# Quad 5 transposed by DMA, quad 8's rows moved into the first out stage, later row copies put behind the value products

## The chip, the cores and the metric

The kernel runs on one core of a Trainium2 chip. The metric is the device time of one launch in microseconds (us). The profile is of one execution: its span is counted from its first to its last instruction, and all times in it count from the start of the span.

## The reference

Eight batches of twelve heads go through a sigmoid attention over 448 positions of 64 values; the heads are put side by side as `x`, and an MLP with a SiLU follows.

```python
def _attn_ref(q, k, v):                     # each (8, 12, 448, 64)
    scores = scale * np.matmul(q, k.transpose(0, 1, 3, 2)) - np.log(S)
    attn = 1.0 / (1.0 + np.exp(-scores))
    return np.matmul(attn, v)

def _moe_ref(x, w_in, w_out):               # x (3584, 768), w_in (768, 2048), w_out (2048, 768)
    h = x @ w_in
    g = h * (1.0 / (1.0 + np.exp(-h)))
    return g @ w_out
```

Inputs and output are float32.

## The kernel before, in words

**Quads.** The work on attention is cut into 24 *quads* of four heads, three to a batch; quads 0 to 5 are batches 0 and 1, and so on. A quad's rows of `q`, `k` and `v` are loaded by POOL with a cast to 16 bits (`load`, L120; the tiles `kf`, `qf` and `vf` have three buffers each, so quad g takes the buffer of quad g - 3). For the scores, `k` and `q` are needed transposed (`kT`, `qT`, three buffers too). There are two ways to that. `pe_transpose` (L188) multiplies 14 blocks of a tensor by the identity on TensorE (PE) and has VectorE (DVE) cast the two PSUM banks, in L203. `dma_transpose` (L207) copies the rows into the order of the tile `kr` or `qr` (L211, on DVE or on POOL) and issues a DMA transpose on SP's queue (L212).

**Units and values.** A *unit* is one of a quad's seven chunks: eight score products of a burst of two units (L225) go into a pair of PSUM banks (`psc`), and ScalarE (ACT) makes the sigmoid `attnT` of them (L232). `values` (L240) multiplies a quad's seven `attnT` by its `v` (`pav`, L256, 28 matmuls), and DVE scales the two banks into `xT` (L267).

**Stages.** The order on every engine is that of the program text; nothing is reordered. In the first stage units 0 to 23 run with the first transposes and values behind them, by the table `behind` (L698). From unit 24 on, bursts of two units stand between stretches of `first_h` (L553), the products `ph` = x·w_in of batches 0 and 1 (L288); for batch 0 ACT takes the sigmoid (L302) and DVE the product into `gTr` (L303), for batch 1 ACT takes a SiLU (L307). After unit 41 the rest of `first_h` runs by itself, up to about 76 us; this part is called the h stage below. There DVE also forms sums of weights (L326, L477) and, by `by_h1`, copies the rows of quads 6, 7 and 8. After quad 8 a small copy on POOL, the *gate*, reads `qT` of quad 8 and so waits until its transpose has landed; behind it in POOL's queue stand the loads of `k` and `q` for quads 9 to 11.

Then an *out stage* and an *h_pair* alternate three times, and a last out stage ends the kernel. Out stage m forms the output of a pair of batches in sets (`out_set`, L487), each of seven products of eight matmuls (L504, called products 1 to 7 of the set, and 8 to 14 those of the next set): DVE makes the sums `S` of two blocks of `gTr` that some products take (L512, L515, L519, L525), reads each product's bank (L514 to L541, L536 and L537 both read product 6) and adds up the results in `osb`, which SP stores. Between the matmuls of a set stand bursts of two or three units of the next six quads, each followed by the values of a finished quad. During attention PSUM has three double pairs in the out stages and two single banks, which `po` takes in turn.

**Row copies in an out stage.** The list `later` holds tensors to be copied and transposed. `rows_if_any` (L591) takes one after each burst and one half way through the products behind it. In the kernel before, a quad is put on the list when the scores of the quad three before it are done (in `burst`, L749). `behind_rows` (L602) then loads the next rows: those that belong to the next stage are held back, and are loaded together behind a gate when the last quad of the stage has been transposed (L610). In h_pair the copies are made by POOL (L811).

**Loads ahead.** `after_transpose` (L635) and `after_values` (L647) issue the loads of later quads and of the weights; `load_w_in` (L150) issues a quarter of `w_in` as four DMAs.

Of the kernel before, what the change touches and what calls it, by code (L numbers as in the profile page):

```python
# [17 lines left out]
def kernel(  # L18
# [9 lines left out]
    nc = tc.nc  # L28
# [13 lines left out]
    NQB = NQ * B  # L42
# [68 lines left out]
    def new_flat(name, g):  # L111
        flat[name, g] = p3.tile([P, 2, NCH, D], F16, tag=f"{name}f", name=f"{name}f")

    def rows_in(name, g):
        b, iq = divmod(g, NQ)
        return source[name][b, 4 * iq : 4 * iq + 4].rearrange(
            "(i h) (p c) d -> (h p) i (c d)", h=2, c=NCH
        )

    def load(names, g, c0=0, c1=NCH):  # L120
        for name in names:
            if (name, g) not in flat:
                new_flat(name, g)
            nc.gpsimd.dma_start(  # L124
                flat[name, g][:, :, c0:c1].rearrange("p i c d -> p i (c d)"),
                rows_in(name, g)[:, :, c0 * D : c1 * D],
            )
# [18 lines left out]
    gate = cpool.tile([1, 1], F16, tag="gate", name="gate")  # L146
# [3 lines left out]
    def load_w_in(step):  # L150
        cols = slice(step * DFF // 4, (step + 1) * DFF // 4)
        rows = moe_w_in[:, cols].rearrange("(iq j h d) f -> h j d iq f", j=2, h=2, d=D)
        for half in range(2):
            for j in range(2):
                nc.gpsimd.dma_start(
                    w_in_sb[j * D : (j + 1) * D, half * NQ : (half + 1) * NQ, cols], rows[half, j]
                )

    def load_w_out(nh, part):
        cols = slice(nh * NO2, (nh + 1) * NO2)  # L160
        fcs = slice(part * NFC // 2, (part + 1) * NFC // 2)
        nc.gpsimd.dma_start(  # L162
            w_out_sb[:, fcs, cols],
            moe_w_out[part * DFF // 2 : (part + 1) * DFF // 2, cols].rearrange(
                "(fc p) e -> p fc e", p=P
            ),
        )

    qkT = {}

    def new_qkT(g):
        for name in ("k", "q"):
            qkT[name, g] = p3.tile([P, NCH, P], F16, tag=f"{name}T", name=f"{name}T")
# [33 lines left out]
    def dma_transpose(g, name, copy):  # L207
        if ("k", g) not in qkT:
            new_qkT(g)
        rows = p2.tile([P, NCH, 2, D], F16, tag=f"{name}r", name=f"{name}r")  # L210
        copy(rows, flat[name, g].rearrange("p j c d -> p c j d"))  # L211
        nc.sync.dma_start_transpose(  # L212
            out=qkT[name, g], in_=rows.rearrange("p c j d -> p (c j d)")
        )
# [3 lines left out]
    def scores(g, ch):  # L218
        attnT[g, ch] = p12.tile([P, 2, S], F16, tag="attnT", name="attnT")
        psc = two_banks("psc")  # L220
        for half in range(2):
            own = slice(half * HP, (half + 1) * HP)
            for j in range(2):
                rows = slice(j * D, (j + 1) * D)
                nc.tensor.matmul(  # L225
                    psc[own, j, :S],
                    qkT["k", g][rows, ch, own],
                    qkT["q", g][rows, :, own],
                    start=True,
                    stop=True,  # L230
                )
        nc.scalar.activation(attnT[g, ch], psc[:, :, :S], AF.Sigmoid, bias=bias_s, scale=QKSCALE)  # L232
# [51 lines left out]
    def h_unit(b, fc):  # L284
        ph = one_bank("ph")
        for at, cc in enumerate(pairs):
            assert b in ready or at < 4
            nc.tensor.matmul(  # L288
                ph[:, :S],
                w_in_sb[:, cc, fc * P : (fc + 1) * P],  # L290
                xT[b][:, cc, :],
                start=(at == 0),
                stop=(at == NCC - 1),
            )
            if at < NCC - 1:
                yield 189
        if fc == NFC - 1:
            h_done.add(b)
        to = gTr[:, fc, first_col(0) + b * S : first_col(0) + (b + 1) * S]
        if b == 0:  # L300
            tsig = room_x()[:, 0]
            nc.scalar.activation(tsig, ph[:, :S], AF.Sigmoid, bias=0.0, scale=ISX)  # L302
            nc.vector.scalar_tensor_tensor(  # L303
                out=to, in0=ph[:, :S], scalar=ISX, in1=tsig, op0=ALU.mult, op1=ALU.mult
            )
        else:
            nc.scalar.activation(to, ph[:, :S], AF.Silu, bias=0.0, scale=ISX)  # L307
        yield 189
# [36 lines left out]
    def x_sums(m, lo, hi):  # L345
        if lo == 0:
            for i in (1, 2, 4):
                tx[m, i] = room_x()
        of = slice(lo, hi)
        x0, x1 = ([xT[2 * m + j][:, c * NQ : (c + 1) * NQ] for c in range(2)] for j in range(2))  # L350
        for o, x, y in (
            (tx[m, 1], x1[0], x0[0]),
            (tx[m, 2], x1[1], tx[m, 1]),
            (x1[0], x1[1], x1[0]),
            (tx[m, 4], x0[1], tx[m, 2]),
        ):
            nc.vector.tensor_sub(o[:, of], x[:, of], y[:, of])
            yield
# [186 lines left out]
            store(rows1, osb[0], whole, (nc.sync, nc.sync))  # L545
        yield 163

    by_h1 = {3: 6, 6: 7, 9: 8}
    early = [h_unit(0, fc) for fc in range(2)]
    sums = w_sums()  # L550
    in_sums = w_in_sums()
# [1 line left out]
    def first_h():  # L553
        for b in range(2):
            for fc in range(NFC):
                yield from early[fc] if b == 0 and fc < 2 else h_unit(b, fc)
                if b == 0 and fc >= 10 or b == 1 and fc < 6:
                    next(in_sums)
                if b == 0:
                    continue  # L560
                if fc >= 2:
                    next(sums)
                if fc in by_h1:
                    for name in ("k", "q"):
                        dma_transpose(by_h1[fc], name, nc.vector.tensor_copy)
                    if by_h1[fc] == 8:

                        nc.gpsimd.tensor_copy(gate, qkT["q", 8][:1, 0, :1])
                        for to in (9, 10, 11):
                            load("kq", to)  # L570

    def sets(m):
        for g in range(0, NCH - 1, 2):
# [12 lines left out]
                kept, row_blocks(m - 1, g), block(m, g), row_blocks(m, g), m == B // 2 - 1  # L586
            )

    later, sums_of_x = [], []

    def rows_if_any(before, copy):  # L591
        if sums_of_x and next(sums_of_x[0], "end") == "end":
# [7 lines left out]
    held = []  # L600

    def behind_rows(g, before):  # L602
        if g + 3 >= NQB:
            return
        if g + 3 < before:
            load("kq", g + 3)
            return
        held.append(g + 3)
        if g + 1 == before:
            nc.gpsimd.tensor_copy(gate, qkT["q", g][:1, 0, :1])  # L610
            for to in held:
                load("kq", to)
            held.clear()
# [21 lines left out]
    def after_transpose(g):  # L635
        if g == 0:
            load("kq", 3)
        elif g == 1:
            load("kq", 4)
            load_w_in(0)  # L640
            load_w_in(1)
        elif g == 2:
            load("kq", 5)
        elif g == 5:
            load("kq", 8)

    def after_values(g):  # L647
        if g == 0:
            load("v", 3)
            load_w_in(2)  # L650
            load_w_in(3)
        elif g == 1:
            load("v", 4)
            load_w_out(0, 0)
            load_w_out(0, 1)
        elif g == 2:
            load("v", 5)
            load_w_out(1, 0)
            load_w_out(1, 1)
            load("kq", 6)  # L660
            load("kq", 7)
        elif g + 3 < NQB:
            load("v", g + 3)
        if g >= 2 * NQ and g % (2 * NQ) == 2 * NQ - 2:
            sums_of_x.append(x_sums(g // (2 * NQ), 0, NQ - 1))

# [17 lines left out]
    def transposes(g, name):  # L684
        pe_transpose(g, ((name, 0, 4), (name, 4, NCH)))
        if name == "q":
            after_transpose(g)

    def rounds(g, end):
        values(g, end)  # L690
        if end == NCH:
            after_values(g)

    def begin(fc, steps):
# [21 lines left out]
        18: ((transposes, 4, "q"),),  # L716
        19: ((rounds, 2, 3),),
        20: ((rounds, 2, 6),),
        21: ((begin, 0, 4),),
        22: ((rounds, 2, 7),),  # L720
        23: ((begin, 1, 4),),
    }
    for n in range(NT_B + 3):
# [16 lines left out]
    def burst(n, size=2):  # L740

        new = units[n : n + size]
        for u in new:
            scores(*u)
        with_values = values_if_any()
        for g, ch in new:
            if ch == NCH - 1:
                waiting.append(g)
                if 9 <= g + 3 < NQB:  # L749
                    later.extend(((g + 3, "k"), (g + 3, "q")))  # L750
        return with_values

    stream = first_h()
    stretch(stream, 1600)
    for n in range(NT_B + 3, 2 * NT_B, 2):
        burst(n)
        if n in (26, 30):
            transposes(5, "k" if n == 26 else "q")
        stretch(stream, 1600)
    values_if_any()  # L760
    for _ in stream:
# [5 lines left out]
    for m in range(B // 2 - 1):  # L767
# [13 lines left out]
        left, n = 0.0, 2 * NT_B * (m + 1)  # L781
# [63 lines left out]
```

## Time and profile before

| what | us |
|---|---|
| median of 3 runs | 368.9 (368.79 to 371.45) |
| the profiled execution, its time | 368.86 |
| its span | 366.9 |
| PE busy (matmuls) | 358.8 |
| DVE busy | 251.8 |
| ACT busy | 250.0 |
| POOL busy | 77.5 |
| units from 24 on with `ph` of batch 0 | 30.45 to 57.1 |
| h stage alone | 57.1 to 76.0 |
| out stage 0 | 76.0 to 123.1 |
| out stage 1 | 156.5 to 211.4 |
| out stage 2 | 244.8 to 292.0 |
| last out stage | 325.6 to the end |

Busy time is the union of an engine's instructions. In the lines of a timeline the columns are start, duration, engine, line, operation, output and inputs, shape and count; a bracket gives the idle time of the engine just before and the instruction that ended it. A line with x2 stands for two instructions, one behind the other. Lines of DMA issues give size and the time from issue to landing. From 18 to 65 us the DMA engines move 204 GB/s on the mean (bytes as written).

### The profile page before, as it was taken

How to read it: one execution, taken by the hardware profiler on the slowest of the kernel's cores; microseconds unless marked ns; L12 is line 12 of the kernel's file. 1: busy time of each engine (PE TensorE's matmuls, PEld its weight loads, DVE VectorE, ACT ScalarE, POOL GpSimd, SP SyncE). 2: the span in 40 equal slices, each digit the busy share in tenths (PEclk: the TensorE clock that was granted, in tenths of full speed). 3: DMA queues.
4: the chain of work that ended last, by engine and by line, in shares of the span. 5: the costliest groups of instructions: out<-in, count | busy, mean ns of one | idle time of the engine just before them, and what ended most of it. 6: DMA issues, size and time to landing. Idle time of an engine off the chain costs nothing.

```text
span 366.9 us, 7595 instructions
## 1 busy us (share of the span) xinstructions
PE 358.8 (98%) x3009; PEld 184.2 (50%) x3009; DVE 251.8 (69%) x458; ACT 250.0 (68%) x339; POOL 77.5 (21%) x116
## 2 busy tenths in 40 slices
PE   7999999999999999999999999999999999999995
PEld 3554445545545555555555555554555555555552
DVE  2565559957756687867675768795756677797763
ACT  4998886479999756687877856679998956640000
POOL 8566521040051082000024046000100000000000
PEclk9999999999999999999999999999999999999998
DMA  8999999987959599006779669902963120003333
GB/s 144 197 204 204 204 204 204 188 120 124 170 86 233 116 128 178 15 0 137 106 136 189 123 135 148 131 2 51 165 100 86 23 67 0 3 0 86 88 87 85
DMA packets 65858, 42.78 MB, mean 117 GB/s; under 512 B 36128, under 2 KB 62496, under 8 KB 65824
## 3 DMA queue, kind: packets, MB, share of 16 engines
q0 software_dynamic: 27072, 22.58, 42.7%
q1 hardware_dynamic: 38320, 19.34, 26.6%
q8 instruction: 23, 0.38, 0.4%
q10 hardware_dynamic: 432, 0.39, 0.3%
q14 instruction: 11, 0.09, 0.1%
HBM read 45.61 MB, written 11.01 MB: 154 GB/s over the span
## 4 chain that ended last, share of the span: by engine, by line
PE 90%; DMA 5%; DVE 2%; POOL 1%; issue 0%; ACT 0%; DVEq 0%
PE po L504 37%; PE psc L225 11%; PE pav L256 8%; PE pa L378 8%; PE pd L378 7%; PE pc L378 7%; PE ph L288 6%; DMA w_out_sb<-in_moe_w_out_dram 5%; PE pb L378 4%; PE pw L183 2%; POOL w_out_sb L162 1%; DVE xT L267 1%; DVE kT L203 1%; PE ptrq L196 1%; PE ptrk L196 0%
## 5 line engine op out<-in xcount | busy, mean ns | idle before, releaser
L232 ACT ACTIVATE attnT<-psc,bias_s 128x896 f16<-128x896 f32 x168 | 157.9, 1010 | 21.7 <-PE psc L225 21.4
L504 PEld LDWEIGHTS <-S 128*128 128x128 f16 x448 | 41.6, 98 | 35.4 <-issue 7.3
L225 PE MATMUL psc<-qT,kT 64*64 64x448 f16 x672 | 50.7, 361 | 1.3 <-ACT attnT L232 0.5
L267 DVE TENSOR_SCALAR xT<-pav 128x448 f16<-128x448 f32 x48 | 27.7, 620 | 29.7 <-PE pav L256 29.7
L124 POOL DMA_DIRECT2D vf<-in_v_dram x24 | 17.2, 717 | 132.3 <-PE pav L256 122.5
L504 PEld LDWEIGHTS <-gTr 128*128 128x128 f16 x336 | 31.2, 98 | 26.6 <-issue 7.9
L504 PE MATMUL po<-T,S 128*128 128x384 f16 x224 | 41.7, 327 | 0.0
L504 PE MATMUL po<-w_out_sb,gTr 128*128 128x384 f16 x224 | 41.5, 327 | 0.0
L378 PEld LDWEIGHTS <-w_in_sb 128*128 128x128 f16 x288 | 27.9, 98 | 26.7 <-issue 1.1
L504 PE MATMUL po<-w_out_sb,S 128*128 128x384 f16 x224 | 40.6, 326 | 0.0
L256 PE MATMUL pav<-attnT,vf 64*64 64x448 f16 x672 | 38.3, 350 | 0.5 <-DVE gTr L303 0.4
L288 PE MATMUL ph<-xT,w_in_sb 128*128 128x448 f16 x192 | 38.7, 353 | 0.1
L378 PE MATMUL pa<-xT,w_in_sb 128*128 128x448 f16 x144 | 33.1, 353 | 0.0
L225 PEld LDWEIGHTS <-kT 64*64 64x64 f16 x672 | 18.0, 104 | 28.7 <-issue 22.4
L378 PEld LDWEIGHTS <-SI 128*128 128x128 f16 x216 | 21.1, 98 | 20.0 <-issue 0.5
L256 PEld LDWEIGHTS <-vf 64*64 64x64 f16 x672 | 21.0, 107 | 13.3 <-issue 3.8
L288 PEld LDWEIGHTS <-w_in_sb 128*128 128x128 f16 x192 | 17.8, 98 | 19.1 <-issue 3.7
L394 ACT ACTIVATE part<-pa 128x448 f32<-128x448 f32 x24 | 13.1, 545 | 18.8 <-PE pa L378 17.9
L504 PE MATMUL po<-T,gTr 128*128 128x384 f16 x112 | 22.1, 327 | 0.0
L372 ACT ACTIVATE gTr<-pc 128x448 f16<-128x448 f32 x24 | 13.1, 545 | 12.8 <-DVE pc L388 12.4
L388 DVE TENSOR_TENSOR part<-pb,part 128x448 f32<-128x448 f32 x24 | 14.9, 621 | 8.3 <-ACT part L394 5.0
L186 ACT ACTIVATE m<-po 128x384 f32<-128x384 f32 x1 | 0.5, 492 | 27.7 <-PE po L504 27.7
(75 smaller groups left out, 468.6 us busy)
## 6 DMA issues: line engine op xcount, KB each, us to landing
out_dram<-osb SPq DMA_DIRECT2D x52, 192.0 KB, 3.0
vf<-in_v_dram POOLq DMA_DIRECT2D x24, 224.0 KB, 7.0
kf<-in_k_dram POOLq DMA_DIRECT2D x23, 224.0 KB, 7.4
qf<-in_q_dram POOLq DMA_DIRECT2D x23, 224.0 KB, 7.7
w_in_sb<-in_moe_w_in_dram POOLq DMA_DIRECT2D x16, 192.0 KB, 7.9
w_out_sb<-in_moe_w_out_dram POOLq DMA_DIRECT2D x4, 768.0 KB, 14.9
out_dram<-osb SPq DMA_DIRECT2D x6, 96.0 KB, 2.1
kT<-kr SPq DMA_TRANSPOSE x18, 3.8
```

Of the source, the lines that this page charges most:

```text
L124: nc.gpsimd.dma_start(flat[name, g][:, :, c0:c1].rearrange("p i c d -> p i (c d)"), rows_in(name, g)[:, :, c0 * D : c1 * D],)
L183: nc.tensor.matmul(pw, dummy[:, :P], dummy, start=True, stop=True)
L225: nc.tensor.matmul(psc[own, j, :S], qkT["k", g][rows, ch, own], qkT["q", g][rows, :, own], start=True, stop=True,)
L232: nc.scalar.activation(attnT[g, ch], psc[:, :, :S], AF.Sigmoid, bias=bias_s, scale=QKSCALE)
L256: nc.tensor.matmul(pav[half][j * D : (j + 1) * D, :S], flat["v", g][own, j, ch, :], at[own, j, :], start=(ch == 0), stop=(ch == NCH - 1),)
L267: nc.vector.tensor_scalar_mul(xT[b][:, half * NQ + iq, :], pav[half][:, :S], SX)
L288: nc.tensor.matmul(ph[:, :S], w_in_sb[:, cc, fc * P : (fc + 1) * P], xT[b][:, cc, :], start=(at == 0), stop=(at == NCC - 1),)
L372: nc.scalar.activation(gTr[:, r * NG + i, col + c * S : col + (c + 1) * S], h, AF.Silu, bias=0.0, scale=ISX)
L378: nc.tensor.matmul(to, w[:, n, i * P : (i + 1) * P], x[:, n], start=(start and n == 0), skip_group_check=not start, stop=(n == NQ - 1),)
L388: nc.vector.tensor_add(o, po, x)
L394: nc.scalar.activation(got[i, 1], bank[i, "a"], AF.Copy)
L504: nc.tensor.matmul(po[:, :NO2], a[:, fc, :], w[:, fc, :], start=(fc == 0), stop=(fc == NHC - 1))
```

## The change

Quad 5 is no longer transposed by PE behind units 26 and 30. Its two loads go out ahead of w_in's second quarter, and its rows are copied by DVE and transposed by DMA behind units 21 and 22. Quad 8 leaves `by_h1`: it stands first on the list `later`, so that its copies, its transposes and then the gate with the loads of quads 9 to 11 come in the first burst of out stage 0. And a quad is put on `later` when the *values* of the quad three before it have been issued, one burst later than before; the row copies then stand behind the two `xT` of that quad on DVE, in most places both in a row.

```diff
-    by_h1 = {3: 6, 6: 7, 9: 8}
+    by_h1 = {3: 6, 6: 7}
...
                         dma_transpose(by_h1[fc], name, nc.vector.tensor_copy)
-                    if by_h1[fc] == 8:
-
-                        nc.gpsimd.tensor_copy(gate, qkT["q", 8][:1, 0, :1])
-                        for to in (9, 10, 11):
-                            load("kq", to)
...
-    later, sums_of_x = [], []
+    later, sums_of_x = [(8, "k"), (8, "q")], []
...
     def behind_rows(g, before):
+        if g == 8:
+            nc.gpsimd.tensor_copy(gate, qkT["q", g][:1, 0, :1])
+            for to in (9, 10, 11):
+                load("kq", to)
+            return
...
         elif g == 1:
             load("kq", 4)
             load_w_in(0)
-            load_w_in(1)
         elif g == 2:
             load("kq", 5)
+            load_w_in(1)
...
         elif g + 3 < NQB:
             load("v", g + 3)
+        if 9 <= g + 3 < NQB:
+            later.extend(((g + 3, "k"), (g + 3, "q")))
...
+    def rows_of_5(name):
+        dma_transpose(5, name, nc.vector.tensor_copy)
+        if name == "q":
+            after_transpose(5)
...
-        21: ((begin, 0, 4),),
-        22: ((rounds, 2, 7),),
+        21: ((rows_of_5, "k"), (begin, 0, 4)),
+        22: ((rounds, 2, 7), (rows_of_5, "q")),
...
             if ch == NCH - 1:
                 waiting.append(g)
-                if 9 <= g + 3 < NQB:
-                    later.extend(((g + 3, "k"), (g + 3, "q")))
...
         burst(n)
-        if n in (26, 30):
-            transposes(5, "k" if n == 26 else "q")
         stretch(stream, 1600)
```

On DVE the order in the first out stage becomes as follows (kr and qr 8, then 9):

```
T, kr, T, L518, L519, qr, L326, L524, ...
... L531, L326, xT x2, kr, qr, L536, L537, L541, ...
```

On SP the transposes of quad 9 stay ahead of the stores of set 1.

## The prediction

> **What bounds the kernel now.** I read the page's shares first, then the waits by engine, then the timelines of PE, DVE, ACT and POOL around the three places that the diff touches.
>
> ```profile
> span 366.9 us, 7595 instructions
> ...
> PE 358.8 (98%) x3009; PEld 184.2 (50%) x3009; DVE 251.8 (69%) x458; ACT 250.0 (68%) x339; POOL 77.5 (21%) x116
> ...
> PEclk9999999999999999999999999999999999999998
> ```
>
> TensorE (PE) is busy for 98% of the span at the full granted clock: time comes only from PE work taken away, and is lost only where PE is made to wait. The profiled execution took 368.86 us, 1.96 more than its span and equal to the median, 368.9. I sum against 368.9. A change under 1%, some 3.7 us, is about what a measurement of this kernel can't tell from none.
>
> All times below are on the clock of the trace of before. Place one, PE timeline, the two bursts with quad 5's transposes (units 26 and 30) and a plain one:
>
> ```profile
> 32.58 0.71 PE L225 MATMUL psc<-qT,kT 64*64 64x448 f16 x8
> 33.22 0.41 PE L196 MATMUL ptrk<-ident,kf 128*64 128x128 f16 x8
> 34.00 0.36 PE L196 MATMUL ptrk<-ident,kf 128*64 128x128 f16 x6 [0.37 <-DVE gTr L303]
> 36.10 0.57 PE L225 MATMUL psc<-qT,kT 64*64 64x448 f16 x8
> ...
> 39.55 0.57 PE L225 MATMUL psc<-qT,kT 64*64 64x448 f16 x8
> 40.05 0.58 PE L196 MATMUL ptrq<-ident,qf 128*64 128x128 f16 x14
> ...
> 42.37 0.57 PE L225 MATMUL psc<-qT,kT 64*64 64x448 f16 x8
> ...
> 51.15 0.57 PE L225 MATMUL psc<-qT,kT 64*64 64x448 f16 x8
> ...
> 53.46 0.57 PE L225 MATMUL psc<-qT,kT 64*64 64x448 f16 x8
> ```
>
> From scores to scores these take 3.52 and 2.82; the plain burst with the same nine ph matmuls takes 2.31. Place two, DVE and then PE, at the end of the first set of the first out stage:
>
> ```profile
> 87.52 1.16 DVE L267 TENSOR_SCALAR xT<-pav 128x448 f16<-128x448 f32 x2 [1.47 <-PE pav L256]
> 88.81 0.56 DVE L536 TENSOR_TENSOR osb<-po,osb 128x384 f32<-128x384 f32 x1
> 89.29 0.55 DVE L537 TENSOR_TENSOR osb<-po,osb 128x384 f32<-128x384 f32 x1
> ```
>
> ```profile
> 90.71 2.11 PE L504 MATMUL po<-w_out_sb,gTr 128*128 128x384 f16 x12
> ```
>
> In an out stage po has two banks, so product 8 (the first of set 2, at 90.71) needs product 6's bank, which L536 and L537 empty by 89.84: 0.87 of slack. Place three, POOL, and the landings of the two loads behind the gate:
>
> ```profile
> 73.57 0.18 POOL L568 COPY gate<-qT 1x1 f16<-1x1 f16 x1 [14.27 <-DMA qT<-qr]
> 74.05 0.72 POOL L124 DMA_DIRECT2D kf<-in_k_dram  x1 [0.30 <-issue]
> 74.76 0.72 POOL L124 DMA_DIRECT2D qf<-in_q_dram  x1
> ```
>
> ```profile
> kf<-in_k_dram POOLq DMA_DIRECT2D x1, 224.0 KB, 4.5
> ...
> qf<-in_q_dram POOLq DMA_DIRECT2D x1, 224.0 KB, 5.0
> ```
>
> Quad 9's rows landed near 79.8, and its copies (L211, at 82.90 and 84.50) found them there.
>
> **Quad 5 by DMA: what it removes.** 28 matmuls and their 0.37 wait: (3.52 - 2.31) + (2.82 - 2.31) = 1.72 us of PE, the upper end. Four casts of about 0.53 leave DVE and two copies (0.61, spaced 0.53) come. Not all of the 1.72 arrives, because scores need one of two psc pairs and ACT frees them (0.92 per attnT, 0.44 per tsig). Followed by hand: burst 28 is due at 34.89, but its second pair is held until 35.42; burst 32 then starts at 41.1 (1.26 early) and burst 36 at 45.75 (1.13 early), where ACT has no gap from 44.60 to 49.5. I take -1.2; ends -1.7 and 0 (ACT takes it all).
>
> **Its cover.** On POOL quad 5's two loads are issued four w_in issues earlier: their rows landed at about 29.55 and 30.64 by the POOL waits that they ended, and come some 3.85 earlier (four pieces of 0.95 each), at 25.7 and 26.8. DVE is free at 25.45, so copy k runs at 25.7; behind it xT of quad 2 isn't due before 27.64. Copy q follows at 28.7. On SP nothing else is queued. The transposes go out near 26.5 and 29.4 and are needed by unit 35 at about 43.3. In quiet they land after 2.9 (at 83.59), beside loads after 7.2 to 11.9 (130.89 to 228.20): 41.3 at the latest. Zero, with 2 us of cover; ends 0 and +4.8 (rival C).
>
> **w_in's second quarter.** Behind two loads of 1.1 each and one transpose its last piece moves from 28.44 to 30.65, and with the transposes, beside which loads ran at about 86 GB/s instead of 204 (six loads, 1.38 MB, from 131 to 147), to about 32.2; by the count of ph matmuls fc 4 needs it at 33.2. The later loads lose about 3.1: (204 - 86)/204 of the 5.3 us that 0.46 MB of transposes take at that rate. The third quarter's last piece (v 3's 32.18 and four pieces) goes from 36.0 to 39.1, due 40.7; v 3 to 34.5, due 35.9; the w_out tiles cost DVE a wait inside the h stage, where it ended 3 us ahead of PE (73.06 against 76.04). Zero; ends 0 and +1.5.
>
> **Quad 8 in the first out stage.** Two copies leave the h stage (hidden there, worth nothing). In the out stage copy k stands ahead of L518 and L519, so L519 ends at 81.24 instead of 80.70; product 4, which reads its S, starts at 81.15. With about 0.1 from DVE's end to PE (the pav at 48.09 came 0.07 after its gTr): +0.25. Copy q starts at 81.16, its transpose goes out at 81.8 and lands, with no load beside it, at 84.7. The gate runs then, and the loads of 9 to 11 follow 0.48 later: kf 9 at 85.2, qf 9 at 85.9. With the landings 4.5 and 5.0 above they are there at 89.7 and 90.9.
>
> **Row copies behind values.** Both copies of quad 9 now stand between xT of quad 6 (done at 88.6 + 0.25) and L536. Copy k waits until 89.7, copy q until 90.9; L536 runs at 91.4 and L537 ends at 92.45; product 8 starts at 92.5 instead of 90.71: 1.8 in all, the 0.25 in it. Queued behind the waiting copies on DVE are L536, L537 and L541, and behind those the stores on SP, which only the osb tiles of set 2 await, later. The nearest landings give the ends: 3.4 (the first loads of the kernel) gives 0.34, 7.4 (the last of the six loads from 74.05) gives 4.2. I take 1.8, since the group of 74.05 is the same six loads on a quiet queue.
>
> The other copies have their rows, and cost only DVE time, 1.06 for a pair. Quad 10: L519 ends at 98.0 for product 11, due 98.1: +0.15. Third stage pair (quads 21 to 23): L537 ends at 259.5 for 259.60, L519 at 266.87 for 267.0: +0.1. Second out stage: xT of quad 12 ends at 173.05, both copies precede L518, and L519 ends at 175.24 where product 11 is due at 174.76: +0.55; quad 16: L528 ends at 180.7 when product 13 is due: +0.05; quad 17, one copy ahead of L519: 190.4 against 190.12: +0.35. Together +0.95, ends 0.3 and 1.5. The gates at 104.66 and 190.12 come up to 6 later, but POOL copies the first of those rows at 128.62 and 216.93, when they have lain there for some 8 us.
>
> Sum: -1.2 + 0 + 1.8 + 0.15 + 0.95 + 0.1 = +1.8; 368.9 + 1.8 = 370.7, its own range 369.6 to 371.9.
>
> The Trainium skill, page "VectorE: DVE Perf Modes", section "The three transpose paths", gives 390 ns on TensorE and 1309 ns by DMA for 128x128, which speaks against moving quad 5. Seven such blocks would be 9.2 us, both tensors in turn 18.3, ending near 44.8 and 1.5 us late: 372.2 by that estimate, a mild case of rival C below. The trace's 2.9 us for a whole seven-block transpose disagrees where DMA is quiet; only its crowded rows come near it.
>
> **The rivals.**
> B, not slower: the loads of quad 9 land in 3.4 us, as the kernel's first one did. Then product 8 loses 0.34: -1.2 + 0.34 + 0.15 + 0.95 + 0.1 = +0.3, 369.2. It decides once qf 9 lands by 89.4. For it: the queue is emptier than at 74. Against it: no pair of loads in the trace did so.
> C: the two transposes stay in flight behind each other beside a full load queue. At the median 8.4 of the crowded rows apiece they end at 26.5 + 16.8 = 43.3, at 10.8 apiece at 48.1, which is 4.8 late. In between, some +2.4: 373.1. For it: DMA is full from 10 to 65 us. Against it: in the crowded rows they overlapped.
> D: the loads of 9 land in 7.4, so product 8 loses 4.2: 370.7 + 2.4 = 373.1. For it: the last loads of the group took that. Against it: its first two didn't.
> E: ACT takes the whole gain: 371.9.
>
> **How the numbers follow.** Forecast 0.5, B 0.17, C 0.11, D 0.11, E 0.11. The likeliest time is 370.7. The range 368.5 to 373.2 holds forecast, B and E, and C and D where they are mild, leaving out under 0.2. Faster by over 1% (below 365.2) needs more than PE's 1.7: 0.02. Slower by over 1% (above 372.6) is most of C and D: 0.2. Within: 0.78.
>
> **What would show it.** No ptr rows for quad 5, and unit 42's scores about 1.2 earlier against their old 78.41; the k and q copies of quad 9 with an idle before them ended by DMA kf and qf; a PE gap at product 8 ended by DVE osb L537; gaps under 0.6 at L519's readers in the second out stage. I am wrong if PE shows no gap at product 8, or one at unit 35 ended by DMA qT.

## The result

| | us |
|---|---|
| before, median of 20 runs (beside after) | 368.73 (368.22 to 371.45) |
| after, median of 20 runs | 371.07 (370.21 to 373.66) |
| ratio | 1.007, 95% interval 1.006 to 1.008 |
| after, the profiled execution | 370.65, its span 368.7 |

The change makes the kernel 2.3 us slower. The forecast was 370.7 within 368.5 to 373.2, with a change of less than 1% as the likeliest case: the time is inside. The prediction took a change under 1% for one that can hardly be told here; with 20 runs of each the interval is 0.1% to either side, so this one can.

The profile page of after, span and busy shares:

```profile
span 368.7 us, 7543 instructions
...
PE 358.5 (97%) x2981; PEld 183.3 (50%) x2981; DVE 250.6 (68%) x456; ACT 249.6 (68%) x339; POOL 77.5 (21%) x116
...
PEclk9999999999999999999999999999999999999999
```

28 matmuls are gone and the clock is granted in full as before (1.000 on the mean, 0.997 before). The busy time of PE falls by 1.0 us up to the h stage, but by only 0.3 in all: in the h stage and in out stages 0 and 1, where the same matmuls run with new waits between them, it is 0.7 longer. The span grows by 1.8. So the cost is in the waits, and the starts of the instructions tell it better than the busy sums. PE's timeline, the lines behind 60 us that have a wait in the bracket (before had none there):

```profile
75.63 2.44 PE L504 MATMUL po<-w_out_sb,gTr 128*128 128x384 f16 x14 [0.63 <-ACT gTr L307]
...
91.75 2.11 PE L504 MATMUL po<-w_out_sb,gTr 128*128 128x384 f16 x12 [1.26 <-DVE osb L537]
...
176.32 1.31 PE L504 MATMUL po<-T,S 128*128 128x384 f16 x7 [0.36 <-DVE S L519]
...
192.06 1.47 PE L504 MATMUL po<-T,S 128*128 128x384 f16 x8 [0.16 <-DVE S L519]
```

The last three are the places that the prediction named. The first, at the very first product of out stage 0, it did not. Set beside the same instructions in before, each line's start tells how far after is ahead or behind by then (`pa`, L378, is the first product of an h_pair, and so marks the end of the out stage ahead of it):

| PE reaches | before | after | after minus before | step |
|---|---|---|---|---|
| scores of unit 24 | 30.45 | 30.45 | 0 | |
| the h stage | 57.08 | 55.87 | -1.21 | -1.21 |
| first product of out stage 0 | 76.04 | 75.63 | -0.41 | +0.80 |
| product 8 | 90.71 | 91.75 | +1.04 | +1.45 |
| end of out stage 0 (first `pa`) | 123.10 | 124.13 | +1.03 | -0.01 |
| first `pa` behind out stage 1 | 211.40 | 213.35 | +1.95 | +0.92 |
| first `pa` behind out stage 2 | 291.99 | 293.93 | +1.94 | -0.01 |

The table explains this one execution, which is 0.4 us faster than the median of its kernel.

Now the chain of product 8. POOL of after, the gate and the two loads of quad 9, and then DVE from the values of quad 6 on:

```profile
84.35 0.18 POOL L599 COPY gate<-qT 1x1 f16<-1x1 f16 x1 [21.59 <-DMA qT<-qr]
84.83 0.71 POOL L124 DMA_DIRECT2D kf<-in_k_dram  x1 [0.30 <-issue]
85.54 0.72 POOL L124 DMA_DIRECT2D qf<-in_q_dram  x1
```

```profile
87.13 1.16 DVE L267 TENSOR_SCALAR xT<-pav 128x448 f16<-128x448 f32 x2 [1.63 <-PE pav L256]
88.66 0.62 DVE L211 COPY kr<-kf 128x896 f16<-128x896 f16 x1 [0.37 <-DMA kf<-in_k_dram]
90.15 0.62 DVE L211 COPY qr<-qf 128x896 f16<-128x896 f16 x1 [0.87 <-DMA qf<-in_q_dram]
90.69 0.55 DVE L536 TENSOR_TENSOR osb<-po,osb 128x384 f32<-128x384 f32 x1
91.15 0.55 DVE L537 TENSOR_TENSOR osb<-po,osb 128x384 f32<-128x384 f32 x1
```

Both copies wait for the landing of their rows (3.8 and 4.6 us after the issue), L536 and L537 stand behind them on DVE, and PE's product 8 starts 0.05 us after L537. This is the chain that the prediction wrote down, link by link. The bracket at PE names only the last link, `osb`; what is late is two engines further back, at the DMA.

### The profile page after: what moved, and what is told of

Read it like the earlier page. It is cut to its first block, busy times and chain, and to the rows that moved or that the text cites. A ratio compares the mean times of both kernels' runs of the same rounds, so it can differ in the third digit from the quotient of the medians.

```text
span 368.7 us, 7543 instructions
## 1 busy us (share of the span) xinstructions
PE 358.5 (97%) x2981; PEld 183.3 (50%) x2981; DVE 250.6 (68%) x456; ACT 249.6 (68%) x339; POOL 77.5 (21%) x116
## 4 chain that ended last, share of the span: by engine, by line
PE 71%; DMA 15%; issue 8%; POOL 3%; DVE 2%; SPq 0%; DVEq 0%; POOLq 0%
PE po L504 32%; PE pa L378 7%; PE pd L378 7%; PE pc L378 7%; PE psc L225 7%; PE pav L256 6%; DMA w_out_sb<-in_moe_w_out_dram 5%; DMA w_in_sb<-in_moe_w_in_dram 5%; PE pb L378 4%; DMA qf<-in_q_dram 3%; POOL kf L124 1%; POOL vf L124 1%; DMA out_dram<-osb 1%; POOL qf L124 1%; DVE S L519 0%
## 5 line engine op out<-in xcount | busy, mean ns | idle before, releaser
L378 PEld LDWEIGHTS <-w_in_sb 128*128 128x128 f16 x288 | 27.9, 98 | 26.7 <-issue 1.1
L378 PE MATMUL pa<-xT,w_in_sb 128*128 128x448 f16 x144 | 33.2, 353 | 0.0
L378 PEld LDWEIGHTS <-SI 128*128 128x128 f16 x216 | 21.1, 98 | 20.0 <-issue 0.5
L124 POOL DMA_DIRECT2D kf<-in_k_dram x25 | 18.2, 728 | 8.8 <-DMA w_out_sb<-in_moe_w_out_dram 3.4
```

The source lines that it names most:

```text
L124: nc.gpsimd.dma_start(flat[name, g][:, :, c0:c1].rearrange("p i c d -> p i (c d)"), rows_in(name, g)[:, :, c0 * D : c1 * D],)
L378: nc.tensor.matmul(to, w[:, n, i * P : (i + 1) * P], x[:, n], start=(start and n == 0), skip_group_check=not start, stop=(n == NQ - 1),)
```

## The experiments

The theory is the prediction's sum with one term added: the early part gives 1.2; 0.8 is lost at the first product, 1.4 at product 8 to the landing of quad 9's rows, 0.9 in the second out stage to the copies ahead of L519. Each run below takes one of these away, or one part of the change alone. Ratios are to before, run on the same chip.

### Quad 5 alone

Before, with only quad 5's part of the diff; quad 8 and the list `later` are as in before.

```diff
         elif g == 1:
             load("kq", 4)
             load_w_in(0)
-            load_w_in(1)
         elif g == 2:
             load("kq", 5)
+            load_w_in(1)
...
-        21: ((begin, 0, 4),),
-        22: ((rounds, 2, 7),),
+        21: ((rows_of_5, "k"), (begin, 0, 4)),
+        22: ((rounds, 2, 7), (rows_of_5, "q")),
...
-        if n in (26, 30):
-            transposes(5, "k" if n == 26 else "q")
```

> The kernel before with the quad 5 part alone (loads ahead of w_in's second quarter, copies and DMA transposes behind units 21 and 22); quad 8 and the later row copies as before. My theory, from the trace of the changed kernel: the h stage starts 1.2 us earlier, but the first product of out stage 0 now takes the PSUM bank that the last ph has just had, and waits some 0.6 to 0.8 for ACT's last SiLU, so that 0.4 is left: about 368.3 against 368.7, and PE shows that gap. Rival: the wait belongs to quad 8's rows in the out stage or to the late copies; then there is no gap and the whole 1.2 arrives: 367.5.

368.87 against 368.58, ratio 1.0009 (0.9999 to 1.0019): no difference that can be told. From the scores of unit 24 to the h stage PE takes 25.43 us instead of 26.63, the whole 1.2 of the forecast. Then it goes again. PE of this run:

```profile
74.89 2.44 PE L504 MATMUL po<-w_out_sb,gTr 128*128 128x384 f16 x14 [0.63 <-ACT gTr L307]
...
78.86 1.31 PE L504 MATMUL po<-T,S 128*128 128x384 f16 x7 [0.60 <-DVE S L515]
...
84.78 0.97 PE L504 MATMUL po<-w_out_sb,S 128*128 128x384 f16 x5 [0.34 <-DVE osb L528]
```

The first gap is the unforeseen one of after, so it belongs to quad 5's part. The other two come of the rows of quad 8, which this kernel still copies in the h stage. DVE:

```profile
72.93 0.62 DVE L211 COPY kr<-kf 128x896 f16<-128x896 f16 x1 [4.11 <-DMA kT<-kr]
```

Quad 8's copy needs the `kr` buffer that quad 6's transpose is still reading. The last load of the early stretch is issued at 63.07 here, in before at 58.58, so the transposes of quads 6 and 7 run beside loads: they hold SP for 3.87 and 3.89 us, where in before each took 1.2 to 1.3. DVE stands still for 4.1 us, and the sums of out stage 0 come late. In after the transposes of quads 6 and 7 are as slow (one of each holds SP for 3.40 and 4.12 us), but no copy of quad 8 stands behind them there. So quad 8's copies were not simply "hidden there, worth nothing" once quad 5 had moved.

### The first product's bank

Why does the first `po` wait for a SiLU? ACT of after, and then of before, at the end of the h stage:

```profile
75.04 0.54 ACT L307 ACTIVATE gTr<-ph 128x448 f16<-128x448 f32 x1 [0.59 <-PE ph L288]
```

```profile
75.11 0.54 ACT L307 ACTIVATE gTr<-ph 128x448 f16<-128x448 f32 x1 [0.59 <-PE ph L288]
76.24 0.55 ACT L307 ACTIVATE gTr<-ph 128x448 f16<-128x448 f32 x1 [0.59 <-PE ph L288]
```

In before the last SiLU (76.24 to 76.79) runs beside the first product (from 76.04). In after, the product starts at 75.63, right behind the last SiLU's end at 75.58: it waits for the bank of the very last `ph`. Which of the four single banks a tile gets is settled when the program is built; with the four `ptr` tiles of quad 5 gone, the order is shifted. As built, the last tiles ahead of out stage 0 lie so (tile and bank):

```
before:  ph 7   ph 6   ph 4   ph 5   po 6
after:   ph 7   ph 4   ph 5   ph 6   po 6
```

To test this, after gets one more tile of a single bank behind unit 38, with one dummy matmul of 64 columns in it:

```diff
     for n in range(NT_B + 3, 2 * NT_B, 2):
         burst(n)
+        if n == 38:
+            pw = one_bank("pw")
+            nc.tensor.matmul(pw[:, :64], dummy[:, :P], dummy[:, :64], start=True, stop=True)
```

> The changed kernel with one PSUM bank more taken behind unit 38 (one matmul of 64 columns on unused data), which turns the order of the single banks: the first product of out stage 0 then takes a bank that was last used four ph earlier, not the one of the very last ph. My theory (the bank's SiLU holds the first product up): the 0.63 gap ended by ACT gTr L307 goes, the stage starts 0.7 to 0.8 earlier against the h stage, and the time falls from 371.1 to about 370.3. Rival (the product waits for ACT for another reason, such as gTr itself): the gap stays and the time with it.

As built, the last `ph` now lies in bank 5 again, and the first `po` takes bank 6. The ACT wait is gone: from the h stage (55.72) to the first product (74.67) PE takes 18.95 us, as in before (18.96), against 19.76 in after. The bank's order is the cause of the 0.80. The total didn't follow: 371.69 (369.62 to 373.41), ratio 1.0084 (1.0053 to 1.0115), where 370.3 was expected. PE shows where the gain stayed in the profiled execution:

```profile
92.28 2.11 PE L504 MATMUL po<-w_out_sb,gTr 128*128 128x384 f16 x12 [2.75 <-DVE osb L537]
```

and DVE why:

```profile
87.87 0.62 DVE L211 COPY kr<-kf 128x896 f16<-128x896 f16 x1 [0.53 <-DMA kf<-in_k_dram]
90.68 0.62 DVE L211 COPY qr<-qf 128x896 f16<-128x896 f16 x1 [2.20 <-DMA qf<-in_q_dram]
```

Its second load was issued at 84.65, 0.9 earlier than in after, and is there at 90.7: 6.0 us, where the same load of the same group took 4.6 in after. So the 0.80 was there up to the load, and a slower landing ate it. That this landing varies by itself is shown below by a kernel that is the same as after up to this point.

### Does ACT hold back the early gain?

The prediction said that 1.72 us of PE go, and took 1.2 as what arrives, since ACT holds back the rest. Before, and quad 5's part alone, each with the sigmoid of batch 0 left out (`gTr` takes the scaled `ph` by one DVE operation), which frees ACT of it:

```diff
-            tsig = room_x()[:, 0]
-            nc.scalar.activation(tsig, ph[:, :S], AF.Sigmoid, bias=0.0, scale=ISX)
-            nc.vector.scalar_tensor_tensor(
-                out=to, in0=ph[:, :S], scalar=ISX, in1=tsig, op0=ALU.mult, op1=ALU.mult
-            )
+            nc.vector.tensor_scalar_mul(to, ph[:, :S], ISX)
```

> The kernel before with batch 0's sigmoid left out (gTr takes the scaled ph by one DVE operation), which frees ACT of 16 times 0.44 us in the stretch of the bursts 24 to 40. It is the base for the next run: I read the time from the scores of unit 24 to the start of the h stage, 26.6 us in the kernel before, and expect about 26.

> The kernel with the quad 5 part alone, and batch 0's sigmoid left out as in the run beside it. With the sigmoid, the removed 1.72 us of PE brought 1.2 on the way from unit 24 to the h stage. My theory: ACT's two sigmoids for the scores and one for ph per burst hold the scores back, so with ACT freed the difference to the run beside this one is the whole 1.6 to 1.7. Rival: the missing 0.5 was lost on PE itself (bank waits, issue), and the difference stays at 1.2.

Neither expectation came true. From unit 24 to the h stage PE takes 25.26 us in the one and 25.17 in the other: 0.09 apart, not 1.6 and not 1.2. The stretches, PE busy in the second column:

```profile
29.75:55.01 25.26, 25.26 (x261) 11.51 (x261) 14.82 (x26) 18.30 (x19) 11.14 (x15) 1.00 1.29 204
```

```profile
30.09:55.26 25.17, 24.36 (x233) 10.77 (x233) 12.50 (x22) 18.53 (x19) 11.11 (x15) 1.00 1.28 194
```

The first is busy throughout. In the second 0.81 of waits for DMA has come in, and these are two lines of its PE:

```profile
43.55 0.38 PE L225 MATMUL psc<-qT,kT 64*64 64x448 f16 x4 [0.62 <-DMA qT<-qr]
...
53.81 1.52 PE L256 MATMUL pav<-attnT,vf 64*64 64x448 f16 x28 [0.19 <-DMA vf<-in_v_dram]
```

The time on PE from the scores of one burst to those of the next shows what happens, burst by burst (in the two right columns ACT is freed):

| burst to burst | before | after | before, freed | quad 5 alone, freed |
|---|---|---|---|---|
| 26 to 28, with the k transposes | 3.52 | 2.45 | 2.97 | 2.45 |
| 28 to 30 | 3.45 | 3.80 | 3.44 | 3.45 |
| 30 to 32, with the q transposes | 2.82 | 2.32 | 2.83 | 2.31 |
| 34 to 36 | 2.39 | 2.42 | 2.45 | 3.13 |

Between the other bursts the kernel with quad 5's transposes on PE and the one without differ by at most 0.02, but for the end of the stretch, where the wait for `vf` shown above comes in.

With ACT freed the 28 matmuls are worth 0.52 each time, 1.04 in all. With the sigmoids their going brings 1.07 and 0.50: 0.55 more went by in burst 26 of before than with ACT freed, 0.37 of it the wait in the bracket there. And 0.35 is lost again from burst 28 to burst 30, where PE of after waits for ACT with the second half of burst 28:

```profile
35.02 0.38 PE L225 MATMUL psc<-qT,kT 64*64 64x448 f16 x4
35.57 0.38 PE L225 MATMUL psc<-qT,kT 64*64 64x448 f16 x4 [0.16 <-ACT attnT L232]
```

With ACT freed this loss is gone, so ACT does hold back a part of the early gain, as the prediction said. The theory of these two runs failed because freeing ACT also takes away this 0.55 of before, and because the run with quad 5's part now waits for its DMA transpose (the 0.68 from burst 34 to burst 36). These are single runs, read by this stretch alone.

### The order of the loads

After, with w_in's second quarter ahead of quad 5's loads again:

```diff
         elif g == 1:
             load("kq", 4)
             load_w_in(0)
+            load_w_in(1)
         elif g == 2:
             load("kq", 5)
-            load_w_in(1)
```

> The changed kernel with w_in's second quarter ahead of quad 5's loads again. My theory: quad 5's k rows land near 29.6 instead of 25.4, DVE's copy k waits for them and holds back xT of quad 2, due at 27.64, to about 30.3; the ph tiles that want its banks wait, so PE shows a gap of 2 to 2.5 us near 29 and the time is about 373 against 371.1 of the changed kernel. Rival: ACT's backlog in this stretch hides the wait: 371.

375.55 (373.87 to 378.37), ratio 1.021 (1.0183 to 1.0237). DVE and then PE:

```profile
29.64 0.62 DVE L211 COPY kr<-kf 128x896 f16<-128x896 f16 x1 [4.39 <-DMA kf<-in_k_dram]
30.18 1.14 DVE L267 TENSOR_SCALAR xT<-pav 128x448 f16<-128x448 f32 x2
```

```profile
30.85 0.35 PE L288 MATMUL ph<-xT,w_in_sb 128*128 128x448 f16 x1 [2.33 <-DVE xT L267]
```

The copy of quad 5 waits for its rows, the values' `xT` stands behind it, and the first `ph` of the stage behind that: 2.5 us with the next line's 0.18. That is what the edit to the loads' order avoids, and it is the expected mechanism. The profiled run, at 373.87 the fastest of the six, is 0.9 above the expectation, and in it product 8 lost 0.5 more than in after. The median is 2.6 above the expectation. The other five have no trace; their mean granted clock is 0.991 to 0.997, against 0.999 in the profiled one. The last section shows that the clock falls in a wait of 5 to 6 us, so such waits are likely in them, but not shown.

### Product 8: the copies' place

After, with quads put on `later` at the scores, as in before:

```diff
         elif g + 3 < NQB:
             load("v", g + 3)
-        if 9 <= g + 3 < NQB:
-            later.extend(((g + 3, "k"), (g + 3, "q")))
...
                 waiting.append(g)
+                if 9 <= g + 3 < NQB:
+                    later.extend(((g + 3, "k"), (g + 3, "q")))
```

> The changed kernel with a quad put on the list when its scores are done, as before, so that quad 9's copies stand ahead of xT of quad 6 again. My theory: copy k waits on DVE from about 82.5 to 88.7 for its rows, with L528 behind it, and product 6, due at 84.3, waits for that bank: a PE gap of 5 to 5.5 us; the second out stage gets its 0.9 back; in all about 374.3. Rival: the copies' place doesn't matter since the rows land for both at the same time and the wait is only moved: 371.

376.33, ratio 1.0207 (1.0193 to 1.0221). DVE and PE:

```profile
88.82 0.62 DVE L211 COPY kr<-kf 128x896 f16<-128x896 f16 x1 [5.99 <-DMA kf<-in_k_dram]
89.35 0.55 DVE L528 TENSOR_TENSOR osb<-po,osb 128x384 f32<-128x384 f32 x1
```

```profile
89.95 1.76 PE L504 MATMUL po<-w_out_sb,S 128*128 128x384 f16 x5 [6.02 <-DVE osb L528]
```

The same copy, one burst earlier, waits the longer for the same landing. So the later row copies don't cause the loss at product 8; they make it smaller, and quad 8's move with the gate behind it is what makes the rows late.

### Product 8: the loads' time

After, with the loads of quads 9 to 11 issued in the h stage with no gate:

```diff
                         dma_transpose(by_h1[fc], name, nc.vector.tensor_copy)
+                if fc == 9:
+                    for to in (9, 10, 11):
+                        load("kq", to)
...
         if g == 8:
-            nc.gpsimd.tensor_copy(gate, qkT["q", g][:1, 0, :1])
-            for to in (9, 10, 11):
-                load("kq", to)
             return
```

> The changed kernel with the loads of quads 9 to 11 issued in the h stage without the gate; quad 8's copies and transposes stay in the first out stage and the copies of quad 9 stay behind xT of quad 6. My theory: product 8's gap (1.42 us against the trace of before) comes from the landing of quad 9's rows; with the rows there it falls to under 0.1: 369.6. Rival: the two copies ahead of L536 and L537 cost it by their DVE time, 1.06, and most of the gap stays: 371.

369.82 (369.71 to 370.23), ratio 1.0036 (1.0024 to 1.0048), as expected. Product 8 has no gap (90.93, DVE's copies wait for nothing), and a smaller one is new on PE. Quad 7's two transposes, which now run beside these loads, hold SP for 5.62 and 3.44 us, in after for 4.12 and 1.29:

```profile
78.63 0.57 PE L225 MATMUL psc<-qT,kT 64*64 64x448 f16 x8 [0.59 <-DMA qT<-qr]
```

The five runs of this kernel lie within 0.5 us of each other, the twenty of after within 3.5. That fits a landing on the path of after, but it is not all: the next kernel has no such wait, and its runs spread by 2.2 us and one more.

Next, after with the gate on quad 7 for quads 9 and 10, so that they go out between the transposes of 7 and of 8; quad 11 stays behind the gate on 8:

```diff
                         dma_transpose(by_h1[fc], name, nc.vector.tensor_copy)
+                if fc == 10:
+                    nc.gpsimd.tensor_copy(gate, qkT["q", 7][:1, 0, :1])
+                    for to in (9, 10):
+                        load("kq", to)
...
             nc.gpsimd.tensor_copy(gate, qkT["q", g][:1, 0, :1])
-            for to in (9, 10, 11):
-                load("kq", to)
+            load("kq", 11)
             return
```

> The kernel after, but quads 9 and 10 are loaded behind a gate on quad 7's transposes (landing near 75), and only quad 11 behind the gate on quad 8. Theory (product 8 waits for nothing but the landing of quad 9's rows, which the gate on quad 8 set): the rows are there by about 81, ahead of their copies at 88, and unlike in the run with the early loads no transpose runs beside them: product 8's gap is gone, no PE wait of another kind comes, and what stays is -1.2 + 0.8 + 0.9 = +0.5: 369.2. Rival (a wait only moves: quad 8's transposes run beside the last of these loads and land late): a PE wait ended by DMA qT at unit 56 or later, 370.5 or more.

369.36 (368.56 to 370.8, and one run of 374.36), ratio 1.0021 (1.0008 to 1.0035): the expected 369.2. The gate opens at 75.80, the rows are there, and product 8 starts at 90.37, 0.34 behind the line ahead of it. What PE waits for behind 60 us is only what the theory leaves: the last SiLU and the two L519.

### The second out stage

After, with quads 15 and later put on `later` at the scores, as in before; quads 9 to 14 as in after.

```diff
-        if 9 <= g + 3 < NQB:
+        if 9 <= g + 3 < 15:
             later.extend(((g + 3, "k"), (g + 3, "q")))
...
                 waiting.append(g)
+                if 15 <= g + 3 < NQB:
+                    later.extend(((g + 3, "k"), (g + 3, "q")))
```

> The changed kernel with quads 15 and later put on the list when the scores of the quad three before are done, as in the kernel before; quads 9 to 11 stay behind values. My theory: the second out stage loses its waits at product 11 (0.5), product 13 (0.06) and at L519's reader of the third set (0.33), so 0.9 less: 370.2. Rival: these waits only eat slack that is lost elsewhere, and nothing changes: 371.1.

371.84 (370.03 to 372.72), ratio 1.0084 (1.0062 to 1.0105), where 370.2 was expected. The two waits for L519 are gone. From the first product of out stage 1 to the first `pa` behind it PE takes 54.88 us (159.03 to 213.91), in before 54.89, in after 55.80: the 0.91 is the copies ahead of L519. The time did not show it. In the profiled execution the second load of quad 9 took 6.1 us here too, and product 8 waited 2.90 instead of 1.26; up to there this kernel is the same as after, so the landing varies from one execution to the next. Of the other executions only the mean granted clock is on record. In this kernel and in the one with the turned banks, three of the six runs have 0.993 to 0.995 and take 372.1 to 373.4, the other three 0.998 to 0.999 and 369.6 to 371.4. The traces with waits of 5.4 and 6.0 us have 0.988 and 0.990, so a still longer wait for this landing is likely in those with the lower clock; no trace shows it.

### All three mended

First try: after with the turned banks, quads 15 and later as in before, and the two copies of quad 9 two bursts later, behind L536 and L537, with the loads left where they are. Beside the two edits above:

```diff
+        if g + 3 == 9:
+            pending.append(9)
-        if 9 <= g + 3 < 15:
+        elif 9 < g + 3 < 15:
             later.extend(((g + 3, "k"), (g + 3, "q")))
...
         new = units[n : n + size]
+        for g in aged:
+            later.extend(((g, "k"), (g, "q")))
+        aged[:] = pending
+        pending.clear()
```

> The changed kernel with three changes: the turned bank order, quads 15 and later as before, and quad 9's copies put on the list two bursts later, so that on DVE they stand behind L536 and L537. My theory: of the terms only the early gain of 1.2 is left, with 0.1 at product 4: about 367.6 against 368.6 of the kernel before. Rival: quad 9's transposes now come too late for unit 63 or the rows' wait on DVE moves to another product: 369 or more.

374.42, ratio 1.0164 (1.015 to 1.0178): the rival came true. Product 8 waits for nothing now, but quad 9's second transpose stands behind a store on SP. SP and then PE:

```profile
89.33 1.75 SPq L212 DMA_TRANSPOSE kT<-kr  x1
91.18 1.29 SPq L497 DMA_DIRECT2D out_dram<-osb  x2
92.56 4.54 SPq L212 DMA_TRANSPOSE qT<-qr  x1
```

```profile
103.58 0.96 PE L225 MATMUL psc<-qT,kT 64*64 64x448 f16 x8 [5.39 <-DMA qT<-qr]
```

PE would be at unit 63, the first of quad 9, at 98.2; the transpose, issued at 92.56 among loads and stores, is there at 103.5, 10.9 us later. A wait of 1.26 us was traded for one of 5.39. So the second try leaves the copies where after has them and moves the loads instead (gate on quad 7), with the turned banks and quads 15 and later as in before.

> The gate on quad 7 of the run before, and with it the turned banks and the copies of quads 15 and later at their old place. Theory: all three losses that were found (0.8 at the first product, 1.4 at product 8, 0.9 in the second out stage) are gone and the early 1.2 stays: 368.7 - 1.2 = 367.5, faster than both. Rival (the time saved ahead of a DMA landing is waited for behind it, as in the two runs with turned banks): 368.7 or more, with a new PE wait ended by a DMA or by osb.

367.77 (367.11 to 368.71) against 368.69, ratio 0.998 (0.9972 to 0.9989): 0.9 faster than before and, by the medians, 3.3 faster than after. That is close to the 367.5 of the theory: of the early 1.2 some 0.9 arrives. Behind 60 us its PE waits for nothing. Its profiled execution is the slowest of its runs, and shows what is left:

```profile
45.23 0.38 PE L225 MATMUL psc<-qT,kT 64*64 64x448 f16 x4 [1.16 <-DMA qT<-qr]
```

Quad 5's second transpose, issued at 29.78, lands 15 us later there. From unit 24 to the h stage PE takes 25.92 there, 0.50 more than in after. So the early gain, too, hangs on a DMA.

## Why the prediction was right, and where it wasn't

| step | predicted | measured |
|---|---|---|
| early gain | -1.2 | -1.21 |
| first product of out stage 0 | not in the sum | +0.80 |
| product 4 | +0.25 | +0.03 |
| product 8, the rest | +1.55 | +1.42 |
| product 11 (quad 10) | +0.15 | 0 |
| second out stage | +0.95 | +0.91 |
| third out stage | +0.1 | 0 |
| sum | +1.8 | +1.95 |

**Product 8** was right in each link. The gate was predicted 8.7 us behind the first product and came 8.7 behind it; the landings were taken as 4.5 and 5.0 and were 3.8 and 4.6. The runs with the copies earlier and with the loads earlier confirm the cause from both sides. What the prediction didn't see is how far this landing varies between executions (4.6 to 6.1 us for one load, and 1.3 to 2.9 us of waiting with it): rival D's 7.4 was not seen in a trace, but the scatter reaches half way to it.

**The second out stage** was right: 0.95 against 0.91, and it vanishes when the copies go back.

**The early gain** was right in size and in its steps. ACT's hold at burst 28 was put to 35.42 and came at 35.57; burst 32 was put to 41.1 and came at 41.14, burst 36 to 45.75 and 45.68. Two sizes were a little off and cancel. The 1.72 is 1.57 by the starts: the plain burst that it subtracts lacks 0.14 by which the scores of burst 26 themselves take longer in both kernels (0.71 instead of 0.57). And ACT held back 0.35, not 0.5.

**The missing step** is the first product. The 28 matmuls and their four casts were counted as time only; their four PSUM tiles went as well, and with them the turn of the banks on which 0.80 us hung. The timeline of before already held the warning: its last SiLU ends 0.75 us after the first product has started, which is free only as long as that product has another bank.

**The small terms** (0.25 at product 4, 0.15, 0.1) were too large by 0.47 together. Each set a DVE end beside a PE start that lay within 0.13 us of it and charged 0.1 to 0.25 for that; PE lost at most 0.03 there. So the total agrees to within 0.4 us partly by luck: 0.80 was missed, and 0.64 was charged too much elsewhere.

**Quad 5's cover** was costed at nothing, "with 2 us of cover". The copies and the issues came when they were forecast (26.13 and 29.35 for the two transposes), but the landings took 11.4 and 13.8 us, the second longer than the 11.9 that was taken for the latest: it landed at 43.15, not by 41.3, just ahead of the burst that needs it (units 34 and 35, at 43.26). So in after the term is nothing, but with under 0.5 us of cover instead of 2. In seven other kernels with quad 5's part PE waits there, by 0.25 to 1.16 us. A wait of 0.72 cost no time (from unit 24 to the h stage 25.48, in after 25.42); the 1.16 cost 0.50. The latest landing is near 45. From the figure of the Trainium skill, page "VectorE: DVE Perf Modes", section "The three transpose paths", 1309 ns for a 128x128 block, the prediction had worked out an end near 44.8 as an estimate, and set it aside by the quiet rows. The landings that the waits show, 43.2 to 45.2, lie near it, though no run here shows that a price per block is the reason: on a quiet queue a tensor's seven blocks took 2.9 us.

Rival B (landing in 3.4) and rival E (ACT takes all) did not happen. Rival C did, in a mild form, in other kernels than after.

## What to carry to other kernels

Taking an instruction away also takes its buffer out of a rotation: look who gets which bank next, and what the last reader of that bank is. A load put behind a gate puts its landing on the path: look at what the waiting copy has behind it on its engine, and expect that the landing varies from run to run (4.6 to 6.1 us here), so that a gain of 0.8 us elsewhere may not be seen in a few runs. When a wait ends at a copy for a DMA, move the load to a quiet stretch rather than the copy: the copy moved back only pushed its transpose into the crowd.

## What the hardware showed that was not expected

**The PE clock falls during a long wait.** The stretches of the run with the copies ahead, from 84 to 96 us, granted clock in the column behind POOL:

```profile
84.00:90.00 6.00, 0.05 (x1) 0.05 (x1) 1.18 (x3) 0.83 (x1) 4.49 (x7) 0.69 0.66 86
90.00:92.00 2.00, 2.00 (x9) 0.69 (x12) 0.84 (x2) 0.00 (x0) 0.00 (x0) 0.50 1.14 160
92.00:94.00 2.00, 2.00 (x36) 0.98 (x28) 1.08 (x3) 1.72 (x2) 0.00 (x0) 0.73 1.24 193
94.00:96.00 2.00, 2.00 (x24) 0.94 (x17) 1.70 (x4) 1.33 (x3) 0.71 (x1) 1.00 1.34 150
```

In the first row, the gap, the clock is 0.69: it falls to 0.50 some 2.3 us after PE's last matmul (83.93). After the gap it is 0.50 for 2 us and at full again by 94: the five matmuls at 89.95 take 1.76 us, where the five at 84.78 in quad 5's run took 0.97. In the 5.4 us gap of the first mended kernel it is the same: it falls some 2.1 us into the gap, and 28 `pav` matmuls behind it take 2.85 us instead of 1.49. In and after the gaps up to 2.9 us it stays at 1.00. By these rows, and the scores and values behind each gap, the waits of 6.0 and 5.4 us cost some 1.5 to 1.8 us more than themselves. The starts agree for the run with the copies ahead: from the first product to the end of out stage 0 PE takes 7.67 us more than in before, of which the gap is 6.02. That is most of why it came out 2 us above its expectation. The Trainium skill, page "TensorE: Matmul & The Clock Gate", section "HAM oscillation — how this bites in real kernels", puts the bound at idle gaps of about 3.4 us; the lengths of the gaps here, none between 2.9 and 5.4, agree with that and can't narrow it. But the clock fell 2.3 and 2.1 us into the two long gaps, while a gap of 2.90 left it at 1.00: a fixed delay from the start of the gap is not what these rows show.

**A DMA transpose beside loads.** On a quiet queue its issue holds SP for 1.2 us and it lands after 2.9. Beside plain loads the same instruction held SP for up to 5.6 us (quad 7's in the run with the early loads) and quad 5's second one landed 13.8 us after its issue in after and 15 in the second mended kernel.
